# Memory attention and a sticky mixture of experts on one Trainium2 core: Phi's maximum spread by a transpose, and a new table of places

## The chip, the core and the metric

The program runs on one core of one Trainium2 chip. A core has engines that work side by side, each through its own list of instructions in order: TensorE (PE, matrix products; its weight loads are shown as PEld), VectorE (DVE), ScalarE (ACT), GpSimd (POOL) and SyncE (SP), which here issues nearly all transfers between main memory and the core. They wait for one another through semaphores. PE reads SBUF, the core's working memory, and writes PSUM, the accumulation memory; ACT and DVE read PSUM, POOL doesn't. The metric is device time in microseconds (us) of one execution.

## The reference, cut to what matters

```python
# attention with a memory: q, k, v [8 batches, 8 heads, 576, 64], phi [8, 8, 576, 32]
a = exp(phi - phi.max(axis=2)); a = a / (a.sum(axis=2) + 1e-9)      # over the 576 tokens
k_m = einsum('bhsm,bhsd->bhmd', a, k); v_m = einsum('bhsm,bhsd->bhmd', a, v)
attn = softmax(q @ k_m.T / 8)                                       # 576 x 32 per head
x = (attn @ v_m), heads side by side                                # [8, 576, 512]
# experts: w_gate [512, 8], w_local [512, 1], w1 [8, 512, 1024], w2 [8, 1024, 512]
for b in batches:
    for s in tokens:
        e = argmax(x[b, s] @ w_gate) if s == 0 or sigmoid(x[b, s] @ w_local) < 0.5 else previous e
        out[b, s] = softmax(x[b, s] @ w_gate)[e] * (relu(x[b, s] @ w1[e]) @ w2[e])
```

The maximum that is taken off Phi runs over the 576 tokens, for each head and memory column. All data are float32.

## The kernel before, in words

Tokens of a batch lie over the 128 partitions: two halves of 64 partitions hold two groups of heads (NG = 2, four heads each, HG = 4), nine tokens to a partition. The work of one batch falls into three parts.

- **Phi's part.** `f_colmax` (L312) takes the maximum over a partition's nine tokens on DVE; `f_pm` (L344) transposes the 128 x 128 result on PE; `f_mc` (L348) reduces it to one number for each column and half, a tile `mc` of 128 x 2; `f_pm2` (L352) brings it back to all partitions: for each half it multiplies `mc`'s column, read 64 times over as the stationary operand, with the identity, which writes 64 partitions of PSUM. `f_cx` (L359) copies the result to SBUF on ACT, `f_sub` takes it off Phi on POOL in two pieces, `f_exp` is ACT's exponential. `f_asum` (L372) adds over a partition's tokens on DVE.
- **Keys, values and scores.** `f_pkv` (L389) multiplies exp(Phi) with keys and values, `f_sums` (L404) with ones; `f_rinv` and `f_kvn` divide, `f_pT` and `f_kvT` transpose, `f_pgg` and `f_ggt` multiply the result into the gate's weights. The queries come in two parts, "a" and "z", of nine blocks of 32 tokens: DVE transposes them (`k_qT`, L474), PE makes the scores (`k_psc`, L499), DVE and ACT the softmax (`k_turn` to `k_mul`), and a transpose on DVE (`k_at`, L553) writes them into `at`, of which there is one buffer; `k_store` stores it to memory (`att_d`).
- **Experts.** The first token's expert is the batch's own: `c_pl` ("pl0", L575) and `c_choice` find it, SP reads its number and loads w1 and w2 in halves of 1 MB, with three buffers. Since x = attn @ v_m, w1 is first multiplied by v_m (`w_pg`, L780, two halves "pg 0" and "pg 1", split into a high and a low part by `w_G`), and the hidden layer is attn times this product (`hidden`, L804): three passes of float32r products on the full array, three buffers of PSUM, ACT's relu and DVE's remainder behind each. `w_split` (L768) splits w2 into high and low parts, on ACT and POOL. `second` (L839) and `second_turned` (L897) make the output, again with three products for each piece. `g_pl` ("g pl", L600) and the steps behind it decide by a scan on DVE which tokens stay with which expert. Tokens with another expert than the batch's first are done in a loop behind all batches (`rest`, L983).

The products use PE's array in different tiles, which the profile prints: 128*128 in `hidden`, `second` and the transposes, 64*32 in pkv, sums, pgg, psc and pg, 128*64 in pm2, 128*32 in g pl, 128*1 in pl0.

**What sets the order.** The schedule is manual: the program is emitted in the order in which the steps are called, and each engine works through its share in this order. The start of the program (`start`, L1145) is written out and holds the first part of batches 0 and 1. After it, the loop at L1235 goes through the experts' products of each batch. Each piece of `hidden`, `second` and `second_turned` yields its length in table time, 37.8 us (END) for a batch; behind each piece the loop emits all steps whose place lies below the time reached, in order of place:

```python
for x in moe(sts[b]):
    now += x
    while places and places[0][0] <= min(now, (b + 1) * END - 0.01):
        _, _, name, n = places.pop(0)
        STEPS[name](sts[n])
```

PLACES (L25 to L111) has 85 rows, one for each kind of step, with a place for each batch; among them are the loads ("phi", "kv", "q", "w1", "w2"), the stores and the splits. A place is table time, which counts the experts' products alone; the steps between take time of their own. So the work on batch b + 1 lies between the products of batch b. A new number changes an engine's list only if the step passes another step of that engine or a piece of the experts' work.

Of the kernel before, what the change touches and what calls it, by code (L numbers as in the profile page):

```python
# [8 lines left out]
F32 = mybir.dt.float32  # L9
F32R = mybir.dt.float32r  # L10
I32 = mybir.dt.int32
AF = mybir.ActivationFunctionType
# [10 lines left out]

END = 37.8
PLACES = {  # L25
    "phi": {2: 1.9, 3: 37.2, 4: 67.4, 5: 94, 6: 129.3, 7: 167.1},
    "kv": {2: 6.06, 3: 36.1, 4: 67.5, 5: 94.1, 6: 129.4, 7: 167.2},
    "colmax": {2: 21.6, 3: 55.3, 4: 80.6, 5: 109.2, 6: 147, 7: 184.8},
# [8 lines left out]
    "asum": {2: 31, 3: 64.8, 4: 92.7, 5: 128.3, 6: 165.5, 7: 203.9},  # L37
    "pkv": {1: 1.56, 2: 34.5, 3: 67.3, 4: 93.6, 5: 128.9, 6: 166.7, 7: 204.5},
    "sums": {1: 3.2, 2: 35.7, 3: 68.6, 4: 94.4, 5: 129.5, 6: 167.8, 7: 205.6},
    "rinv": {1: 3.2, 2: 35.8, 3: 69.6, 4: 95.1, 5: 131.3, 6: 169.1, 7: 207.8},  # L40
    "kvn": {1: 7.7, 2: 36.8, 3: 70.1, 4: 95.5, 5: 131.7, 6: 170, 7: 208.2},
    "pT": {1: 9.2, 2: 38, 3: 71.6, 4: 97.5, 5: 133.7, 6: 171.5, 7: 209.3},
    "kvT": {1: 9.8, 2: 38.3, 3: 71.9, 4: 97.5, 5: 133.7, 6: 171.5, 7: 209.3},
    "kv store": {0: 18.79, 1: 11.1, 2: 41.9, 3: 73.7, 4: 98.7, 5: 136.3, 6: 174.1, 7: 211.9},
    "pgg": {1: 9.9, 2: 39.5, 3: 73.1, 4: 99, 5: 135.8, 6: 173, 7: 210.8},
    "ggt": {1: 9.9, 2: 41.6, 3: 73.2, 4: 99.7, 5: 135.9, 6: 173.7, 7: 211.5},
# [15 lines left out]
    "choice": {1: 22.1, 2: 53.4, 3: 86.6, 4: 112.5, 5: 150.3, 6: 187.5, 7: 227.3},  # L62
    "expert": {1: 22.3, 2: 53.9, 3: 87.6, 4: 112.7, 5: 150.5, 6: 187.7, 7: 227.5},
# [36 lines left out]
    "store": {0: 39.3, 1: 79.4, 2: 116.9, 3: 153.6, 4: 189.4, 5: 227.2, 6: 265},  # L100
    "pairs": {0: 29.3},
    "list": {7: 278.9},
# [8 lines left out]
}  # L111


# [1 line left out]
def tile_memattn_stickymoe(  # L115
# [12 lines left out]
    nc = tc.nc  # L128
    B, H, S, D = q.shape
    M = phi.shape[3]  # L130
    E, DM, F = w1.shape
    P = 128
    HG = 4
    NG = H // HG
# [10 lines left out]
    psml = ctx.enter_context(tc.tile_pool(name="psml", bufs=2))  # L145
# [9 lines left out]
    ident = const.tile([P, P], F32, name="ident")  # L155
# [192 lines left out]
    def f_mc(st):  # L348
        st.mc = psml.tile([P, NG], F32, tag="mc", name="mc")
        nc.vector.tensor_reduce(out=st.mc, in_=st.pm.rearrange("x (g p) -> x g p", g=NG), axis=AX.X, op=ALU.max)  # L350

    def f_pm2(st):  # L352
        st.pm = ps_a.tile([P, P], F32, tag="pa", name="pm")
        for g in range(NG):
            nc.tensor.matmul(
                st.pm[half[g]], lhsT=st.mc[:, g : g + 1].to_broadcast([P, D]), rhs=ident, start=True, stop=True
            )
# [678 lines left out]
    a, z = PARTS  # L1036
# [15 lines left out]
    def al(st, p):  # L1052
# [8 lines left out]
        "colmax": f_colmax,  # L1061
        "pm": f_pm,
        "mc": f_mc,
        "pm2": f_pm2,
        "cx": f_cx,
        "sub 0": lambda st: f_sub(st, 0),
# [78 lines left out]
    def start():  # L1145
# [14 lines left out]
        f_pm(s)  # L1160
        warm(1)
        f_mc(s)
        f_pm2(s)
        warm(14)
        f_cx(s)
# [28 lines left out]
        f_pm(n)  # L1194
        warm(3)
        f_mc(n)
        c_pl(s)
        c_choice(s)
# [5 lines left out]

        k_psc(s, p)
        f_pm2(n)
        f_cx(n)
        f_sub(n, 1)
# [23 lines left out]
    with tc.manual_schedule():  # L1232
        start()
        places = sorted((x, i, name, n) for i, (name, row) in enumerate(PLACES.items()) for n, x in row.items())
        for b in range(B):  # L1235
            now = b * END
# [38 lines left out]
```

## Time and profile before

| | |
|---|---|
| median of 3 runs | 417.17 us (416.37 to 418.63) |
| profiled execution | 416.56 us, its span 414.8 us |
| PE | busy 395.0 us, 95% of the span, 4195 products |
| PE weight loads | 326.7 us, 79% |
| DVE | 284.4 us, 69%, 714 instructions |
| ACT | 177.8 us, 43%, 427 instructions |
| POOL | 150.9 us, 36% |
| DMA | 82.58 MB, 199 GB/s on average |
| chain that ended last | PE 79%, DMA 11%, DVE 5% of the span |
| clock granted to PE | 0.999 of full speed |

In the rows of the timeline the first two numbers are the start, in us from the span's start, and the length of an instruction (or of a run of equal ones, with their count behind "x"). Then come the engine, the line of the kernel, the operation, "out<-in", for PE the tile of the array, and the shape. A bracket gives the engine's idle time before it and what ended it. "SPq" is SP's queue, whose instructions issue transfers. Matmuls of PE overlap, and their ends are modelled; the distance from one start to the next says more than the length. Rows of stages give a stretch, its length, then for each engine the busy time and the number of instructions.

### The profile page before, as it was taken

Reading aid. Unit: us, or ns where it says so; the run is one execution under the profiler, and the core shown is the slowest. Engines: PE = TensorE matmul, PEld = TensorE weight load, DVE = VectorE, ACT = ScalarE, POOL = GpSimd, SP = SyncE. Lnnn points to the kernel's source line nnn. Section 1 sums busy time; section 2 is a strip of 40 time slices with the busy share of each in tenths; the row PEclk is TensorE's granted clock in tenths of the full one; section 3 lists DMA queues with packets and bytes.
Section 4 is the critical chain, followed back from the end, with each engine's and each line's share of the span. In section 5 each row is a group of like instructions: output and inputs, shape, how many; then the busy total and the mean of one; then the engine's idle time right before and its main releaser. Section 6 shows DMA issues by size and latency. Waiting matters only on the chain.

```text
span 414.8 us, 10606 instructions
## 1 busy us (share of the span) xinstructions
PE 395.0 (95%) x4195; PEld 326.7 (79%) x4195; DVE 284.4 (69%) x714; ACT 177.8 (43%) x427; POOL 150.9 (36%) x162
## 2 busy tenths in 40 slices
PE   8778898999999989999999999999999999999994
PEld 2546866798777977699778997789878996899884
DVE  4487788878976797886759767777757676625300
ACT  2154652436442744435541564336541564146010
POOL 3024541536241744038510681029410660156000
PEclk9999999999999999999999999999999999999999
DMA  8969793999197939798789198965974087202011
GB/s 238 286 224 291 167 372 122 199 283 378 31 351 127 371 131 246 174 379 299 228 162 399 37 300 152 297 244 164 241 134 170 2 246 253 82 0 65 25 40 55
DMA packets 115445, 82.58 MB, mean 199 GB/s; under 512 B 69616, under 2 KB 89088, under 8 KB 115392
## 3 DMA queue, kind: packets, MB, share of 16 engines
q1 hardware_dynamic: 115328, 81.84, 66.4%
q8 instruction: 35, 0.57, 0.6%
q14 instruction: 18, 0.15, 0.1%
q0 software_dynamic: 64, 0.02, 0.1%
HBM read 66.60 MB, written 15.24 MB: 197 GB/s over the span
## 4 chain that ended last, share of the span: by engine, by line
PE 79%; DMA 11%; DVE 5%; issue 1%; SPq 1%; ACT 1%; DVEq 0%
PE ph L819 22%; PE po L907 8%; PE po L857 8%; PE po L908 7%; PE po L909 7%; PE po L859 7%; PE po L858 7%; DMA att_d<-at 6%; DMA kv_t<-in_v_dram 5%; PE pkv L396 4%; PE pg L787 3%; PE psc L507 2%; PE pl L604 1%; DVE h L829 1%; PE po L881 1%
## 5 line engine op out<-in xcount | busy, mean ns | idle before, releaser
L777 POOL TENSOR_TENSOR w2l<-raw,w2h 128x512 fp32r<-128x512 f32 x64 | 82.0, 1303 | 31.2 <-ACT w2h L776 23.5
L819 PE MATMUL ph<-ah,Gh 128*128 128x256 f32 (+1 forms) x256 | 74.5, 306 | 1.4 <-DVE h L829 1.3
L829 DVE SCALAR_TENSOR_TENSOR h<-ph,h 128x320 fp32r<-128x320 f32 (+2 forms) x104 | 52.7, 519 | 31.9 <-ACT h L827 31.5
L819 PE MATMUL ph<-ah,Gl 128*128 128x256 f32 (+1 forms) x256 | 71.6, 295 | 0.0
L907 PE MATMUL po<-h,w2l 128*128 128x320 f32 x224 | 71.5, 319 | 0.0
L909 PE MATMUL po<-h,w2h 128*128 128x320 f32 x224 | 69.2, 309 | 0.0
L908 PE MATMUL po<-h,w2h 128*128 128x320 f32 x224 | 69.2, 309 | 0.0
L827 ACT ACTIVATE h<-ph 128x320 fp32r<-128x320 f32 (+1 forms) x96 | 46.4, 489 | 44.7 <-PE ph L819 44.4
L857 PE MATMUL po<-w2h,h 128*128 128x512 f32 (+1 forms) x152 | 60.7, 399 | 0.0
L914 POOL TENSOR_TENSOR oT<-oT,gT 128x320 f32<-128x320 f32 x28 | 20.7, 741 | 104.3 <-DVE oT L913 97.4
L859 PE MATMUL po<-w2h,h 128*128 128x512 f32 (+1 forms) x152 | 57.8, 380 | 0.0
L858 PE MATMUL po<-w2l,h 128*128 128x512 f32 (+1 forms) x152 | 57.7, 379 | 0.0
L819 PE MATMUL ph<-al,Gh 128*128 128x256 f32 (+1 forms) x256 | 54.8, 295 | 0.0
L819 PEld LDWEIGHTS ph<-ah,Gh 128*128 128x128 f32 x256 | 48.1, 188 | 7.6 <-issue 3.6
L819 PEld LDWEIGHTS ph<-ah,Gl 128*128 128x128 f32 x256 | 48.2, 188 | 0.0
L563 POOL TENSOR_TENSOR al<-at,ah 128x576 fp32r<-128x576 f32 (+1 forms) x18 | 23.1, 1289 | 64.7 <-ACT ah L559 42.8
L907 PEld LDWEIGHTS po<-h,w2l 128*128 128x128 f32 x224 | 42.0, 188 | 5.6 <-issue 5.2
L776 ACT ACTIVATE w2h<-raw 128x512 fp32r<-128x512 f32 x64 | 38.4, 625 | 11.9 <-PE po L909 10.1
L908 PEld LDWEIGHTS po<-h,w2h 128*128 128x128 f32 x224 | 42.1, 188 | 0.2
L909 PEld LDWEIGHTS po<-h,w2h 128*128 128x128 f32 x224 | 42.1, 188 | 0.0
L819 PEld LDWEIGHTS ph<-al,Gh 128*128 128x128 f32 x256 | 41.1, 188 | 0.1
L857 PEld LDWEIGHTS po<-w2h,h 128*128 128x128 f32 x152 | 28.6, 188 | 14.3 <-issue 9.4
(153 smaller groups left out, 578.6 us busy)
## 6 DMA issues: line engine op xcount, KB each, us to landing
raw<-in_moe_w_dram SPq DMA_DIRECT2D x34, 512.0 KB, 6.2
raw<-in_moe_w_dram SPq DMA_DIRECT2D x15, 1024.0 KB, 6.9
kv_t<-in_k_dram SPq DMA_DIRECT2D x7, 1152.0 KB, 8.7
kv_t<-in_v_dram SPq DMA_DIRECT2D x7, 1152.0 KB, 11.2
q_t<-in_q_dram SPq DMA_DIRECT2D x112, 72.0 KB, 3.3
att_d<-at SPq DMA_DIRECT2D x8, 576.0 KB, 9.8
out_dram<-oT SPq DMA_DIRECT2D x28, 160.0 KB, 5.6
out_dram<-ot SPq DMA_DIRECT2D x17, 256.0 KB, 6.0
```

The source lines that it names most:

```text
L563: (eng or nc.gpsimd).tensor_tensor(out=st.al[:, gs, ss], in0=st.at[:, gs, ss], in1=st.ah[:, gs, ss], op=ALU.subtract)
L776: nc.scalar.activation(h, src, AF.Copy)
L777: nc.gpsimd.tensor_tensor(out=l, in0=src, in1=h, op=ALU.subtract)
L819: nc.tensor.matmul(pv[:, c - c0], lhsT=lt[:, g, cs], rhs=rt[:, g, s0 : s0 + n], start=(i == 0), stop=(i == 5),)
L827: nc.scalar.activation(hc[:, :, 0:n], pv, AF.Relu)
L829: nc.vector.scalar_tensor_tensor(out=hc[:, :, o : o + z - a], in0=pv[:, :, a:z], scalar=0.0, in1=hc[:, :, a:z], op0=ALU.max, op1=ALU.subtract,
L857: nc.tensor.matmul(po[:, c0:c1], lhsT=h[:, c, th], rhs=hi, start=(c == 0), stop=False)
L858: nc.tensor.matmul(po[:, c0:c1], lhsT=h[:, c, th], rhs=lo, start=False, stop=False)
L859: nc.tensor.matmul(po[:, c0:c1], lhsT=h[:, c, tl], rhs=hi, start=False, stop=(c == FC - 1))
L907: nc.tensor.matmul(po[:, 0:n], lhsT=lo, rhs=h[:, c, 0:n], start=(c == 0), stop=False)
L908: nc.tensor.matmul(po[:, 0:n], lhsT=hi, rhs=h[:, c, 0:n], start=False, stop=False)
L909: nc.tensor.matmul(po[:, 0:n], lhsT=hi, rhs=h[:, c, n : 2 * n], start=False, stop=(c == FC - 1))
```

## The change

Two things are changed.

The spread of Phi's maximum, in batches 1 to 7: `f_mc` adds an activation that writes `mc`'s two columns 64 times each into a tile `mcw` of 128 x 128, and `f_pm2` transposes it by one product on the full array, where it had two products on an array tile of 128*64 (four instructions of PE). Batch 0 keeps the old way.

```diff
     def f_mc(st):
         st.mc = psml.tile([P, NG], F32, tag="mc", name="mc")
         nc.vector.tensor_reduce(out=st.mc, in_=st.pm.rearrange("x (g p) -> x g p", g=NG), axis=AX.X, op=ALU.max)
+        if st.b:
+            st.mcw = psml.tile([P, NG, D], F32, tag="mcw", name="mcw", bufs=1)
+            nc.scalar.activation(st.mcw, st.mc.unsqueeze(2).to_broadcast([P, NG, D]), AF.Copy)
 
     def f_pm2(st):
         st.pm = ps_a.tile([P, P], F32, tag="pa", name="pm")
+        if st.b:
+            nc.tensor.transpose(st.pm, st.mcw.rearrange("x g p -> x (g p)"), ident)
+            return
         for g in range(NG):
             nc.tensor.matmul(
                 st.pm[half[g]], lhsT=st.mc[:, g : g + 1].to_broadcast([P, D]), rhs=ident, start=True, stop=True
             )
```

The table PLACES: 61 of the 85 rows get new numbers, many of them changed by a few tenths. The rows that move products of PE, loads, or steps which the text below speaks of:

```diff
-    "kv": {2: 6.06, 3: 36.1, 4: 67.5, 5: 94.1, 6: 129.4, 7: 167.2},
+    "kv": {2: 6.06, 3: 36.1, 4: 74.8, 5: 98.6, 6: 133.9, 7: 171.7},
-    "pkv": {1: 1.56, 2: 34.5, 3: 67.3, 4: 93.6, 5: 128.9, 6: 166.7, 7: 204.5},
-    "sums": {1: 3.2, 2: 35.7, 3: 68.6, 4: 94.4, 5: 129.5, 6: 167.8, 7: 205.6},
+    "pkv": {1: 1.52, 2: 34.49, 3: 70.3, 4: 93.6, 5: 127.71, 6: 165.81, 7: 204.5},
+    "sums": {1: 1.52, 2: 34.49, 3: 70.3, 4: 94.4, 5: 127.71, 6: 165.81, 7: 204.51},
-    "pgg": {1: 9.9, 2: 39.5, 3: 73.1, 4: 99, 5: 135.8, 6: 173, 7: 210.8},
+    "pgg": {1: 9.9, 2: 39.5, 3: 73.1, 4: 100.59, 5: 138.8, 6: 176, 7: 213.8},
-    "pl0": {1: 20, 2: 53.3, 3: 86.6, 4: 111.6, 5: 149.4, 6: 186.6, 7: 226.4},
+    "pl0": {1: 20, 2: 54.8, 3: 86.6, 4: 111, 5: 148.8, 6: 186, 7: 225.8},
-    "z psc": {1: 24.2, 2: 51.9, 3: 88.3, 4: 119.4, 5: 157.2, 6: 190.5, 7: 232.8},
+    "z psc": {1: 24.2, 2: 53.29, 3: 89, 4: 119.4, 5: 157.2, 6: 190.5, 7: 232.8},
-    "at store": {0: 8.78, 1: 31.2, 2: 67.5, 3: 91.6, 4: 140.3, 5: 179.9, 6: 211.4, 7: 253.7},
+    "at store": {0: 6.78, 1: 33.2, 2: 67.5, 3: 91.6, 4: 140.3, 5: 179.9, 6: 211.4, 7: 253.7},
-    "w2 0": {1: 22.7, 2: 57.9, 3: 93.2, 4: 121.1, 5: 161.2, 6: 199, 7: 235.9},
+    "w2 0": {1: 22.7, 2: 57.9, 3: 93.2, 4: 122, 5: 162.1, 6: 199.9, 7: 236.8},
-    "pg 1": {0: 0.13, 1: 32.7, 2: 71.5, 3: 97.6, 4: 132.9, 5: 170.1, 6: 205.9, 7: 242.8},
-    "G 1": {0: 0.13, 1: 32.8, 2: 71.6, 3: 98.3, 4: 135, 5: 171.1, 6: 206.9, 7: 244.1},
+    "pg 1": {0: 0.51, 1: 34.5, 2: 71.5, 3: 97.6, 4: 132.9, 5: 165.81, 6: 213.79, 7: 246.79},
+    "G 1": {0: 0.51, 1: 34.78, 2: 71.6, 3: 98.3, 4: 135, 5: 171.1, 6: 213.79, 7: 246.79},
```

The rows "pm", "mc", "pm2", "g pl" and "q" keep their places, and the splits of batch 6 move back by up to 4.5 us. The loads of w1 keep theirs but for batch 2 (1.5 us later).

More of the change, by code (lines that the diff above doesn't have):

```diff
@@ L25 @@
 PLACES = {
-    "phi": {2: 1.9, 3: 37.2, 4: 67.4, 5: 94, 6: 129.3, 7: 167.1},
-    "kv": {2: 6.06, 3: 36.1, 4: 67.5, 5: 94.1, 6: 129.4, 7: 167.2},
-    "colmax": {2: 21.6, 3: 55.3, 4: 80.6, 5: 109.2, 6: 147, 7: 184.8},
+    "phi": {2: 1.3, 3: 37.2, 4: 70.3, 5: 94, 6: 129.3, 7: 167.1},
+    "kv": {2: 6.06, 3: 36.1, 4: 74.8, 5: 98.6, 6: 133.9, 7: 171.7},
+    "colmax": {2: 21.6, 3: 55.3, 4: 80, 5: 109.8, 6: 147.6, 7: 185.4},
     "pm": {2: 24.1, 3: 59.1, 4: 84.8, 5: 114, 6: 151.8, 7: 189.6},
@@ L31 @@
     "pm2": {2: 27.1, 3: 60.6, 4: 89.4, 5: 117.2, 6: 155, 7: 192.8},
[3 rows of a table removed]
[3 rows of a table added]
     "exp 0": {2: 29.4, 3: 63.8, 4: 90.5, 5: 125.6, 6: 163.7, 7: 201.5},
     "exp 1": {2: 30.9, 3: 63.8, 4: 91.4, 5: 126.8, 6: 164.6, 7: 202.4},
-    "asum": {2: 31, 3: 64.8, 4: 92.7, 5: 128.3, 6: 165.5, 7: 203.9},
-    "pkv": {1: 1.56, 2: 34.5, 3: 67.3, 4: 93.6, 5: 128.9, 6: 166.7, 7: 204.5},
-    "sums": {1: 3.2, 2: 35.7, 3: 68.6, 4: 94.4, 5: 129.5, 6: 167.8, 7: 205.6},
-    "rinv": {1: 3.2, 2: 35.8, 3: 69.6, 4: 95.1, 5: 131.3, 6: 169.1, 7: 207.8},
@@ L41 @@
-    "kvn": {1: 7.7, 2: 36.8, 3: 70.1, 4: 95.5, 5: 131.7, 6: 170, 7: 208.2},
+    "asum": {2: 31, 3: 64.8, 4: 92.7, 5: 127.71, 6: 165.5, 7: 203.9},
+    "pkv": {1: 1.52, 2: 34.49, 3: 70.3, 4: 93.6, 5: 127.71, 6: 165.81, 7: 204.5},
+    "sums": {1: 1.52, 2: 34.49, 3: 70.3, 4: 94.4, 5: 127.71, 6: 165.81, 7: 204.51},
+    "rinv": {1: 2.9, 2: 35.8, 3: 70.3, 4: 95.1, 5: 131.3, 6: 169.1, 7: 207.8},
+    "kvn": {1: 7.4, 2: 36.8, 3: 70.3, 4: 95.5, 5: 131.7, 6: 170, 7: 208.2},
     "pT": {1: 9.2, 2: 38, 3: 71.6, 4: 97.5, 5: 133.7, 6: 171.5, 7: 209.3},
-    "kvT": {1: 9.8, 2: 38.3, 3: 71.9, 4: 97.5, 5: 133.7, 6: 171.5, 7: 209.3},
@@ L44 @@
-    "kv store": {0: 18.79, 1: 11.1, 2: 41.9, 3: 73.7, 4: 98.7, 5: 136.3, 6: 174.1, 7: 211.9},
-    "pgg": {1: 9.9, 2: 39.5, 3: 73.1, 4: 99, 5: 135.8, 6: 173, 7: 210.8},
-    "ggt": {1: 9.9, 2: 41.6, 3: 73.2, 4: 99.7, 5: 135.9, 6: 173.7, 7: 211.5},
+    "kvT": {1: 9.8, 2: 38, 3: 71.9, 4: 97.5, 5: 133.7, 6: 171.5, 7: 209.3},
+    "kv store": {0: 18.79, 1: 11.1, 2: 41.9, 3: 76, 4: 98.7, 5: 136.3, 6: 174.1, 7: 211.9},
+    "pgg": {1: 9.9, 2: 39.5, 3: 73.1, 4: 100.59, 5: 138.8, 6: 176, 7: 213.8},
+    "ggt": {1: 9.9, 2: 41.6, 3: 75.5, 4: 100.59, 5: 138.8, 6: 176, 7: 213.8},
@@ L47 @@
     "q": {1: 1.15, 2: 22.6, 3: 59.6, 4: 88.7, 5: 124.3, 6: 162.1, 7: 199.9},
[3 rows of a table removed]
[3 rows of a table added]
     "a turn": {1: 14.1, 2: 46.1, 3: 75.6, 4: 103.2, 5: 141.3, 6: 178.8, 7: 217.7},
[2 rows of a table removed]
[2 rows of a table added]
     "a exp": {1: 15.2, 2: 49.8, 3: 80.8, 4: 104.7, 5: 142.8, 6: 180.3, 7: 219.2},
     "a sum": {1: 17.6, 2: 49.8, 3: 82, 4: 105.8, 5: 143.9, 6: 181.4, 7: 220.3},
[3 rows of a table removed]
[3 rows of a table added]
     "a ah": {1: 18.8, 2: 52.8, 3: 85.1, 4: 108.9, 5: 147, 6: 183.9, 7: 223.4},
[2 rows of a table removed]
-    "choice": {1: 22.1, 2: 53.4, 3: 86.6, 4: 112.5, 5: 150.3, 6: 187.5, 7: 227.3},
-    "expert": {1: 22.3, 2: 53.9, 3: 87.6, 4: 112.7, 5: 150.5, 6: 187.7, 7: 227.5},
[18 rows of a table removed]
[2 rows of a table added]
@@ L82 @@
+    "choice": {1: 22.1, 2: 54.9, 3: 86.6, 4: 111.3, 5: 149.1, 6: 186.3, 7: 226.1},
+    "expert": {1: 22.3, 2: 55.4, 3: 87.6, 4: 112.7, 5: 150.5, 6: 188, 7: 227.5},
[18 rows of a table added]
     "pg 0": {1: 30.7, 2: 66.7, 3: 96.2, 4: 127.7, 5: 165.8, 6: 203.6, 7: 240.5},
[3 rows of a table removed]
[3 rows of a table added]
     "g pl": {0: 4.27, 1: 30.9, 2: 61.6, 3: 93.6, 4: 132, 5: 169.8, 6: 207.1, 7: 246.8},
[3 rows of a table removed]
[3 rows of a table added]
     "g exp": {0: 9.2, 1: 33, 2: 65.7, 3: 96.3, 4: 135.3, 5: 173.1, 6: 210.9, 7: 250.1},
```

82 rows, old and new, of the table PLACES are left out of this document.

## The prediction

> **What bounds the kernel now.** I read the page first, then a table of the engines' busy time by stage, then the timeline of TensorE (PE) around each small product, and last the rows of what PE waits for.
>
> ```profile
> span 414.8 us, 10606 instructions
> ```
>
> The profiled execution took 416.56 us: this span and 1.76 us around it. The stages, cut where a batch's expert begins (columns: span, PE, weight loads, DVE, ACT, POOL busy, granted clock, DMA share, GB/s):
>
> ```profile
> 38.60:88.80 50.20, 46.77 (x524) 38.22 (x518) 40.49 (x105) 22.04 (x57) 20.34 (x24) 1.00 0.80 212
> 187.90:234.60 46.70, 46.70 (x510) 39.71 (x509) 35.03 (x84) 21.30 (x52) 18.56 (x17) 1.00 0.77 239
> ```
>
> In the later batch PE is busy for all 46.70 us; in the first it waits for 3.4 of 50.2. From then on PE's own order is the time: what shortens PE's list shortens the run, unless another engine comes late for it. Up to there it is otherwise:
>
> ```profile
> 63.21 0.78 DVE L555 STREAM_TRANSPOSE at<-sc 128x576 f32<-128x576 f32 x1 [0.94 <-DMA att_d<-at]
> ```
> ```profile
> 64.13 0.24 PE L578 MATMUL pl<-ggt,at 128*1 128x8 f32 x4 [1.11 <-DVE at L555]
> ```
>
> PE stands 1.11 us before batch 1's pl0, because the transpose into `at` waits for the store of batch 0's `at`. In SP's queue this store keeps its neighbours under the new table. So what PE gains before 64 us is lost in that wait, and a loss of up to 1.11 us there is hidden too. I count nothing before 64 us.
>
> **The change part by part.** First the spread of Phi's maximum, before: four products on an array tile of 128*64, inside full-array products of 256 columns.
>
> ```profile
> 191.90 0.40 PE L819 MATMUL ph<-al,Gh 128*128 128x256 f32 x2
> 192.22 0.44 PE L355 MATMUL pm<-ident,mc 128*64 128x128 f32 x4
> 192.59 0.39 PE L819 MATMUL ph<-ah,Gh 128*128 128x256 f32 x1
> 192.82 0.28 PE L819 MATMUL ph<-ah,Gl 128*128 128x256 f32 x1
> ```
>
> The nearest row to the transpose that replaces them is the transpose of the column maxima, the same 128x128 on the full array:
>
> ```profile
> 188.83 0.28 PE L819 MATMUL ph<-ah,Gl 128*128 128x256 f32 x1
> 188.95 0.40 PE L819 MATMUL ph<-al,Gh 128*128 128x256 f32 x2
> 189.19 0.27 PE L346 MATMUL pm<-ident,cm 128*128 128x128 f32 x1
> 189.21 0.36 PE L819 MATMUL ph<-ah,Gh 128*128 128x256 f32 x1
> 189.41 0.28 PE L819 MATMUL ph<-ah,Gl 128*128 128x256 f32 x1
> ```
>
> I count starts, since matmuls overlap: 188.83 to 188.95 gives 0.12 for one of these products. From 191.90 to 192.82 are three such steps, 0.35, in 0.92: the spread costs 0.57. From 188.95 to 189.41 are three in 0.46: the transpose costs 0.11. The difference is 0.46 a batch. Six batches (2 to 7) lie behind 64 us: 6 x 0.46 = 2.8. The other end takes the transpose by its duration of 0.27, 0.30 a batch and 1.8 in all; I take 2.8, because the cost in a stream is what the neighbours' starts show. Batch 1's spread lies in the start, ahead of the wait above, and counts for nothing.
>
> The Trainium skill, "TensorE: Matmul & The Clock Gate", Part 4: PE-mode transpose, gives about 275 ns for a 128x128 transpose inside a kernel, mostly access latency. The row's duration of 0.27 agrees with it, the starts beside it do not pay it; by that figure the sum would lose 1.0.
>
> Second, the table. Where steps now stand together I need the price of a product that stands alone. Batch 2's pkv and sums apart:
>
> ```profile
> 83.30 2.25 PE L396 MATMUL pkv<-kv_t,phi_t 64*32 64x128 f32 x144
> 85.48 0.41 PE L907 MATMUL po<-h,w2l 128*128 128x320 f32 x1
> ...
> 86.32 0.31 PE L909 MATMUL po<-h,w2h 128*128 128x320 f32 x1
> 86.56 0.27 PE L407 MATMUL pkv<-ones,asum 64*32 64x1 f32 x16
> 86.75 0.41 PE L907 MATMUL po<-h,w2l 128*128 128x320 f32 x1
> 87.00 0.30 PE L908 MATMUL po<-h,w2h 128*128 128x320 f32 x1
> 87.15 0.31 PE L909 MATMUL po<-h,w2h 128*128 128x320 f32 x1
> ```
>
> and batch 5's pg 0 alone, then its pkv and sums, which already adjoin:
>
> ```profile
> 204.54 0.39 PE L859 MATMUL po<-w2h,h 128*128 128x512 f32 x1
> 204.86 1.09 PE L787 MATMUL pg<-raw,kvT 64*32 64x512 f32 x16
> 205.88 0.50 PE L857 MATMUL po<-w2h,h 128*128 128x512 f32 x1
> 206.22 0.39 PE L858 MATMUL po<-w2l,h 128*128 128x512 f32 x1
> 206.44 0.40 PE L859 MATMUL po<-w2h,h 128*128 128x512 f32 x1
> ...
> 207.46 2.25 PE L396 MATMUL pkv<-kv_t,phi_t 64*32 64x128 f32 x144
> 209.45 0.29 PE L407 MATMUL pkv<-ones,asum 64*32 64x1 f32 x16
> 209.68 0.50 PE L857 MATMUL po<-w2h,h 128*128 128x512 f32 x1
> ```
>
> Sums alone: 86.32 to 87.00 is 0.68, less two steps of 0.15 (87.00 to 87.15), so 0.39. Pkv alone runs 2.18 to the next product, pkv with sums 2.22: there sums cost 0.04. Adjoining saves 0.35, for two changes of array tile less. Pg alone: 204.54 to 206.22 is 1.68, less two steps of 0.23 (206.22 to 206.44), so 1.22, of which 1.02 is its own pace (204.86 to 205.88); at least 0.20 lies in its two changes. One change costs 0.10 to 0.175.
>
> The Trainium skill, "TensorEngine Tiling (Array Packing)", Tiling Modes, Key Properties, says that changing the tiling mode drains the engine and that changing the tile alone doesn't. The 0.39 against 0.04 agrees.
>
> I ordered both tables by their numbers, as the loop at the end of the program does, and counted changes of array tile on PE behind batch 1's pl0: 118 before, 93 after. Twelve go with the spread, already counted. Four go with sums 2 and 3 that join pkv: 2 x 0.35 = 0.7. Nine go elsewhere: pg 1 of batch 1 behind pkv and sums (2), pg 0 of batches 4 and 5 ahead of pkv (4), pg 1 of batches 5 and 6 moved from g pl to pkv or pgg (1 each), pg 1 of batch 7 to g pl (1). Nine at 0.10 to 0.175 are 0.9 to 1.6; I take 1.2, the middle, since pg stands between the two rows in size. Sums.1 joins too, but ahead of 64 us.
>
> Third, what the change adds: one activation a batch, and a link in the chain mc, mcw, pm2, cx. Batch 3 has the shortest of these links:
>
> ```profile
> 114.96 0.23 DVE L350 TENSOR_REDUCE mc<-pm 128x2 f32<-128x128 f32 x1
> ```
> ```profile
> 115.69 0.44 PE L355 MATMUL pm<-ident,mc 128*64 128x128 f32 x4
> ```
> ```profile
> 115.80 0.69 ACT L944 ACTIVATE ot<-po,gt 128x512 f32<-128x512 f32 x1 [3.38 <-PE po L859]
> 116.38 0.27 ACT L361 ACTIVATE cx<-pm 128x128 f32<-128x128 f32 x1
> ```
>
> The widened copy has the shape of cx's, 0.27. ACT stands idle for 3.38 before 115.80, so mcw can run from 115.19 to 115.46, ahead of PE's 115.69. What is queued behind it on ACT is the eviction of ot, whose products end after it. With the handing over I charge 0.2 for all six. In batches 4 to 7 relus and splits are queued behind mcw, and PE waits for relus only through three buffers of PSUM: no charge, unless mc itself is late (below).
>
> Fourth, moved steps on other queues. The kv loads of batches 4 to 7 are issued 4.5 to 7.3 us later by the table, behind stores and w2 loads; pkv 4 still stands 18.8 us behind its load, and the landing takes:
>
> ```profile
> kv_t<-in_v_dram SPq DMA_DIRECT2D x7, 1152.0 KB, 11.2
> ```
>
> so nothing is charged. For batches 6 and 7 q goes ahead of w2 0 in SP's queue. That bears on batch 6's pl0, where the same wait as at 64 us recurs:
>
> ```profile
> 247.69 12.78 SPq L253 DMA_DIRECT2D q_t<-in_q_dram  x16
> ```
> ```profile
> 278.87 0.78 DVE L555 STREAM_TRANSPOSE at<-sc 128x576 f32<-128x576 f32 x1 [1.74 <-DMA att_d<-at]
> ```
> ```profile
> 279.71 0.24 PE L578 MATMUL pl<-ggt,at 128*1 128x8 f32 x4 [0.52 <-DVE at L555]
> ```
>
> Sixteen issues of q take SP 12.78, and the store of `at` comes behind them. Started earlier, they let that store out earlier. pl0 itself moves one step of 0.88 ahead (six products of 0.147 by the program's own yield). Between a gain of 0.52 and a loss of 0.88 I take a gain of 0.4: DVE is ready 1.74 before the store lets it go on, so a store that comes earlier by that much leaves room for both moves.
>
> The sum: 2.8 + 0.7 + 1.2 + 0.4 - 0.2 = 4.9. 416.56 - 4.9 = 411.7. The median of the runs, 417.17, lies 0.6 above the profiled one; the sum from there gives 412.3. I say 412.0.
>
> **Rivals.** *Only the removed products count.* If a transpose costs its 0.27 and a change of tile beside pg nothing, 1.8 + 0.7 - 0.2 = 2.3 is left: 416.56 - 2.3 = 414.3. For it: durations are what the rows print. Against it: the two starts around 189.2.
>
> *The saved time turns into waits.* If DVE or the store of `at` sets each batch's pace, PE only waits longer at pl0, or for relus' buffers; what is saved behind the last such wait at 279.7 remains: batch 7's spread 0.46 and two changes of tile, 0.3; 416.56 - 0.8 = 415.8, no change. For it: both waits for that store, and DVE's 40.49 of 50.20 in the early stage. Against it: from 187.9 PE has no idle time, and DVE only 35.03 of 46.70.
>
> *Slower: PE stands at pm2 for mcw.* ACT takes its list in order, and mcw comes behind whatever the table has put there:
>
> ```profile
> 189.94 1.14 ACT L776 ACTIVATE w2h<-raw 128x512 fp32r<-128x512 f32 x2
> ```
>
> With two splits ahead (1.14) and then its own 0.27, the copy would come 1.4 late where nothing is to spare, and PE would stand for it in each of six batches: 8.4 against 4.9, 416.56 + 3.5 = 420.1. It decides from 4.9/6 = 0.8 of mean wait at pm2. Against it: between 115.19 and 115.69 ACT was idle.
>
> **How the numbers follow.** About 0.5% (2.1 us) is what a measurement of this kernel can tell from no change. Forecast 0.62, only-removed 0.12, waits 0.17, slower 0.09. The first two are faster by over 0.5%, the second narrowly: 0.74. The waits are no change: 0.17. Slower: 0.09. The range goes down to 408.0, where each change of tile costs 0.175 (0.4 more) and PE's idle time of 3.4 in the first stage goes as well; up to 416.5 it holds the rival of less gain and most of the one of the waits.
>
> **What would show it.** Right: pm2 as one transpose, 0.1 between its neighbours' starts; sums 2 and 3 directly behind pkv; PE's busy time down by about 5 and its idle time unchanged; stages from 187.9 on at 46.0 or less. Wrong: PE idle at pm2 with ACT as releaser, longer waits at pl0 for `at`, or pg behind pkv still paying its 0.2. A change of more than 2 us in the first 64 us would break my claim that nothing counts there.

## The result, and the profile after

The changed kernel takes 412.19 us (median of 7 executions, 411.31 to 414.49), the kernel before beside it 417.17 (7 executions, 416.32 to 418.93). The ratio is 0.9882, with a 95% interval of 0.9848 to 0.9917: faster by 1.2%. The prediction was 412.0, within 408.0 to 416.5. The profiled execution of the changed kernel took 414.21, near the upper end of its own executions, so the two traces lie only 2.4 apart; a second trace, taken below, took 412.06.

The page of the changed kernel, span and PE's busy time:

```profile
span 412.4 us, 10572 instructions
...
PE 391.7 (95%) x4170; PEld 327.3 (79%) x4174; DVE 284.2 (69%) x714; ACT 179.4 (44%) x434; POOL 151.3 (37%) x162
```

PE's busy time fell by 3.3 (395.0 before; 391.3 in the second trace), where the prediction said about 5. Busy time is a poor witness here: a group of products that stands waiting in its middle, as some below, is partly counted as busy.

The spread of batch 5 in the changed kernel, on PE's timeline:

```profile
190.51 0.40 PE L825 MATMUL ph<-al,Gh 128*128 128x256 f32 x2
190.75 0.27 PE L358 MATMUL pm<-ident,mcw 128*128 128x128 f32 x1
190.77 0.36 PE L825 MATMUL ph<-ah,Gh 128*128 128x256 f32 x1
190.97 0.28 PE L825 MATMUL ph<-ah,Gl 128*128 128x256 f32 x1
191.09 0.28 PE L825 MATMUL ph<-ah,Gh 128*128 128x256 f32 x1
```

By the starts: 190.51 to 190.97 is 0.46 for three products of 0.12 (190.97 to 191.09) and the transpose, so the transpose costs 0.10. The prediction took 0.11 from the neighbour's row, and 0.57 for the old spread. The Trainium skill's figure in "TensorE: Matmul & The Clock Gate", Part 4: PE-mode transpose, some 275 ns (measured with bfloat16 data), is again the row's duration and not what the stream pays.

Batch 2's pkv with sums, and pg 1 of batch 1 behind them:

```profile
82.31 2.25 PE L402 MATMUL pkv<-kv_t,phi_t 64*32 64x128 f32 x144
84.30 0.25 PE L413 MATMUL pkv<-ones,asum 64*32 64x1 f32 x12
84.39 0.61 PE L793 MATMUL pg<-raw,kvT 64*32 64x512 f32 x1
...
84.49 1.14 PE L793 MATMUL pg<-raw,kvT 64*32 64x512 f32 x15
85.56 0.42 PE L913 MATMUL po<-h,w2l 128*128 128x320 f32 x1
```

The three follow one another with no product of the experts between them. To price such a block I use one rule from here on: from the start of the last full-array product ahead of it to the start of the second one behind it, less the steps these two take in a run of their own. This block costs 3.45 by that rule. In the kernel before, pkv cost 2.38, sums 0.39 and pg about 1.22 apart.

The wait at batch 1's pl0 on the timeline of the changed kernel, and the stage of batch 3's experts (columns as in the prediction):

```profile
63.88 0.78 DVE L561 STREAM_TRANSPOSE at<-sc 128x576 f32<-128x576 f32 x1 [1.81 <-DMA att_d<-at]
...
64.80 0.24 PE L584 MATMUL pl<-ggt,at 128*1 128x8 f32 x4 [1.20 <-DVE at L561]
```
```profile
186.57:233.51 46.94, 46.50 (x506) 39.98 (x505) 35.51 (x86) 21.60 (x53) 19.68 (x18) 1.00 0.84 256
```

The wait at pl0 stayed (1.11 before, 1.20 now), as forecast. But the stage from 186.57 takes 46.94, longer than its 46.70 before, though PE's list in it is shorter: a wait has appeared that the prediction does not name. The experiments trace it.

### The profile page after: what moved, and what is told of

Its sections match the earlier page's. It is cut to its first block, busy times and chain, and to the rows that moved or that the text cites. A ratio compares the mean times of both kernels' runs of the same rounds, so it can differ in the third digit from the quotient of the medians.

```text
span 412.4 us, 10572 instructions
## 1 busy us (share of the span) xinstructions
PE 391.7 (95%) x4170; PEld 327.3 (79%) x4174; DVE 284.2 (69%) x714; ACT 179.4 (44%) x434; POOL 151.3 (37%) x162
## 4 chain that ended last, share of the span: by engine, by line
PE 68%; DMA 11%; SPq 11%; DVE 6%; issue 2%; ACT 1%; DVEq 0%; ACTq 0%
PE ph L825 19%; SPq L253 7%; PE po L863 7%; PE po L913 7%; PE po L865 6%; PE po L864 6%; PE po L915 6%; PE po L914 6%; DMA att_d<-at 6%; PE pkv L402 3%; PE pg L793 3%; DMA raw<-in_moe_w_dram 3%; DMA kv_t<-in_v_dram 2%; PE psc L513 2%; DVE h L835 1%
```

## The experiments

Twelve runs were made, in four sets, each set beside the kernel before on one chip. "Profiled" is the one execution that left the trace.

| kernel | median, us (executions) | ratio to before, 95% interval | profiled |
|---|---|---|---|
| spread alone | 416.14 (12) | 0.9978, 0.9951 to 1.0004 | 418.12 |
| table alone | 413.75 (6) | 0.9905, 0.9869 to 0.9942 | 413.70 |
| widened copy four times | 416.06 (12) | 0.9961, 0.9935 to 0.9986 | 416.91 |
| one small product for each group | 437.10 (2) | 1.0472, 1.0350 to 1.0594 | 435.96 |
| one full-array product for each group | 422.53 (2) | 1.0123, 1.0020 to 1.0227 | 422.98 |
| eight small products for each group | 455.99 (2) | 1.0925, 1.0781 to 1.1069 | 454.33 |
| whole change again | 411.59 (5) | 0.9857, 0.9834 to 0.9881 | 412.06 |
| loads behind the store of `at` | 410.51 (6) | 0.9846, 0.9812 to 0.9881 | 410.91 |
| the same, maximum of batch 4 in halves | 410.82 (5) | 0.9843, 0.9817 to 0.9869 | 414.71 |
| pkv 3 at its old place | 414.73 (8) | 0.9948, 0.9920 to 0.9976 | 414.79 |
| spread alone, again | 416.25 (10) | 0.9979, 0.9957 to 1.0002 | 415.57 |
| before, again | 416.25 (1) | | 416.25 |

The standing theory was the prediction's: PE's own list is the time, the spread gives 2.8 of it, the table 1.9, and the added link costs 0.2 at most. The rivals: waits eat the gain, or PE stands at pm2 for the copy.

### The two parts apart, and the link lengthened

The spread alone, with the old table:

```diff
+        if st.b:
+            st.mcw = psml.tile([P, NG, D], F32, tag="mcw", name="mcw", bufs=1)
+            nc.scalar.activation(st.mcw, st.mc.unsqueeze(2).to_broadcast([P, NG, D]), AF.Copy)
...
+        if st.b:
+            nc.tensor.transpose(st.pm, st.mcw.rearrange("x g p -> x (g p)"), ident)
+            return
```

> The spread by a transpose alone, with the old table. By the prediction's sum (0.46 a batch, six batches behind 64 us, less 0.2 for the longer chain) it gains 2.6 us on the kernel before. If a transpose costs its duration of 0.27, it gains 1.6. If saved time of PE only turns into waits, it gains less than 0.8.

A miss: 416.14 against 417.33 beside it, 1.2 in place of 2.6, and the interval takes in no change.

The table alone is the changed kernel without these lines.

> The new table alone, with the old spread. By the prediction's sum (0.7 for sums 2 and 3, 1.2 for nine changes of array tile, 0.4 for batch 6's pl0) it gains 2.3 us. If a change of tile beside pg costs nothing, it gains 0.7. The trace of the changed kernel still has PE waiting 0.75 at batch 6's pl0, so that I now expect 1.9 without the 0.4.

Also a miss, to the other side: 413.75 against 417.33, 3.6 faster.

The link made longer: the widened copy is written four times over in place of once.

```diff
-            nc.scalar.activation(st.mcw, st.mc.unsqueeze(2).to_broadcast([P, NG, D]), AF.Copy)
+            for _ in range(4):
+                nc.scalar.activation(st.mcw, st.mc.unsqueeze(2).to_broadcast([P, NG, D]), AF.Copy)
```

> The changed kernel with the copy into mcw done four times, so that the link from mc to the transpose is 0.9 us longer in every batch. By the prediction the link has room: in the changed kernel's trace the transpose starts 0.16 behind the copy in batch 3, 0.78 in batch 5, 0.83 in batch 6 and more elsewhere, so that PE stands 0.8 in batch 3, 0.1 to 0.2 in batches 5 and 6: about 1 us slower than the changed kernel. If the link sets the time (the slower rival), 0.9 in each of six batches, 5.6 us slower.

It took 416.06, about 4 above the changed kernel: more than the 1 of the first case, less than the 5.6 of the second. Its timeline at batch 3's spread:

```profile
114.39 1.33 ACT L354 ACTIVATE mcw<-mc 128x128 f32<-128x128 f32 x4 [2.81 <-DVE mc L350]
...
115.78 0.33 PE L359 MATMUL pm<-ident,mcw 128*128 128x128 f32 x1 [0.75 <-ACT mcw L354]
```

and the same place in the changed kernel:

```profile
114.68 0.31 ACT L353 ACTIVATE mcw<-mc 128x128 f32<-128x128 f32 x1 [2.79 <-DVE mc L350]
...
115.15 0.27 PE L358 MATMUL pm<-ident,mcw 128*128 128x128 f32 x1
```

One copy ends at 114.99, 0.16 ahead of the transpose: PE does not wait, but there is no more room than that. With 0.93 more (three copies of 0.31) the starts around pm2 lengthen by 1.0, 0.6, 0.3 and 0.3 in batches 3 to 6, and not in 2 and 7. So the six links have room for one copy, not for four. These 2.2 are about half of the 4. The rest, against the second trace of the changed kernel (below), is waiting of PE at other places, which no theory had named yet: batch 6's pl0, behind the store of `at`, costs 2.30 by the starts in place of 0.72, and the scores of batches 4 and 5 cost 0.4 and 0.3 more.

### What a change of array tile costs

96 products that nobody reads, of one column, each ahead of a group of `hidden` products (whose first product overwrites what they wrote):

```diff
+                for _ in range(1):
+                    nc.tensor.matmul(ph[0:32, 0:1], lhsT=wz[0:64, 0:32], rhs=wz[0:64, 0:1], start=True, stop=True)
```

> The changed kernel with one product of no use ahead of each group of the hidden layer (96 in all): bfloat16 zeros, one column, on an array tile of 64*32, into a bank of PSUM that the group's own first product overwrites. If a change of array tile costs 0.10 to 0.175 us, each pays two: 96 x 0.20 to 0.35 = 19 to 34 us slower than the changed kernel. If the cost is the product's own, it is what the next kernel's full-array product costs.

> The same with the product of no use on the full array, one column too, so that no tile changes. If changes of tile are the cost, this adds only the product and its weight load, below 0.1 each, under 10 us in all. If small products as such are the cost, it adds as much as the small tile did.

> The same with eight products on the 64*32 tile ahead of each group: 768 products, but no more changes of tile than with one. If the change is the cost, it adds at 0.01 for each further product (the pace of pkv's products) 96 x 7 x 0.01 = 7 us to what one does; all eight take the same tile, so that up to 0.1 each, 67 us, is possible where one waits for the other. If each small product pays by itself, it adds eight times what one does.

The second has `ph[0:128, 0:1]`, `wz[0:128, 0:128]` and `wz[0:128, 0:1]`, so the full array; the third has eight of the small ones in place of one. Against the changed kernel's 412.19 (measured in another set; the kernel before beside it was at 417.17, here at 416.89) the first is slower by 24.9, which is 0.26 for each small product, the second by 10.3, 0.11 for each. The third adds 18.9 to the first for 672 more products, 0.028 each. Timelines of the first and the second:

```profile
240.07 0.31 PE L917 MATMUL po<-h,w2h 128*128 128x320 f32 x1
240.31 0.17 PE L822 MATMUL ph<-wz 64*32 64x1 bf16 x1
240.41 0.39 PE L827 MATMUL ph<-ah,Gh 128*128 128x256 f32 x1
240.63 0.28 PE L827 MATMUL ph<-ah,Gl 128*128 128x256 f32 x1
```
```profile
240.94 0.40 PE L827 MATMUL ph<-al,Gh 128*128 128x256 f32 x2
241.18 0.18 PE L822 MATMUL ph<-wz 128*128 128x1 bf16 x1
241.21 0.39 PE L827 MATMUL ph<-ah,Gh 128*128 128x320 f32 x1
241.45 0.31 PE L827 MATMUL ph<-ah,Gl 128*128 128x320 f32 x1
```

Ahead of the small product PE loses 0.24 to its start in place of 0.15, and the first product behind it takes 0.22 in place of 0.12. Behind the full-array one the follower starts 0.03 later, and its own step takes 0.24 in place of 0.15. By the starts in the three traces the medians are 0.30 for a small product, 0.12 for a full-array one and 0.025 for a further small one, so the times of two executions each are not far off. A small product that follows another small one costs almost nothing; if it would cost as little alone, a pair of changes is 0.26 - 0.03 = 0.23, 0.115 for each (0.14 by the starts), within the prediction's 0.10 to 0.175. If one takes off what the full-array product costs, which changes no tile, it is 0.15, 0.075 for each (0.09 by the starts), below that range. That a change costs something is shown; its size only between these two. The rule of the Trainium skill, "TensorEngine Tiling (Array Packing)", Key Properties, that a change of mode drains the engine, agrees with 0.26 against 0.028; it states no price.

### The whole again, and the first 64 us

The changed kernel again, and two edits of it that aim at two waits in its trace. First, the loads of batch 2's Phi, keys and values go behind the store of batch 0's `at` in SP's queue, and the store of batch 5's goes earlier:

```diff
-    "phi": {2: 1.3, ...
-    "kv": {2: 6.06, ...
+    "phi": {2: 6.85, ...
+    "kv": {2: 6.9, ...
-    "at store": {..., 5: 179.9, ...
+    "at store": {..., 5: 169, ...
```

> The changed kernel once more, beside the two below. 5.0 us faster than before, and in the trace the waits of the first 64 us and at batch 6's pl0 again, if they belong to the order and not to one execution.

> The changed kernel with the store of at ahead of phi 2 and kv 2 (batch 0) and ahead of w2 1 and kv 7 (batch 5) in SP's queue. If PE's waits at pl0 of batches 1 and 6 are waits for that store behind other transfers, both go: 1.36 - 0.10 and 0.75 - 0.10, together up to 1.9 us faster than the changed kernel. If something else comes as late (the scores' chain on DVE, 0.9 before the store in batch 1), 0.9 at most at the first.

The whole took 411.59. The edit took 410.51, faster by 1.1 by medians where up to 1.9 was hoped for, and the intervals overlap. In its trace the wait is gone; SP's rows, and DVE and PE:

```profile
48.02 0.41 SPq L578 DMA_DIRECT2D att_d<-at  x1
48.52 0.38 SPq L231 DMA_DIRECT2D phi_t<-in_phi_dram  x1
```
```profile
61.69 0.78 DVE L561 STREAM_TRANSPOSE at<-sc 128x576 f32<-128x576 f32 x1
...
63.26 0.25 PE L584 MATMUL pl<-ggt,at 128*1 128x8 f32 x4
```

The store left 2.1 earlier than in the trace of the whole (50.15), DVE no longer waits for it, and the block of pl0 costs 0.37 in place of 1.58 by the starts. So the prediction's cause of that wait is right, and in the block it was worth 1.2. Batch 6's pl0, for which the store of batch 5 was moved, costs 0.37 in place of 0.72. How much of this the whole run keeps, the medians do not settle: the first 64 us of one kernel alone, to the mark used below, moved by 2.3 between two executions (spread alone). Second, the same with the maximum of batch 4 (2.25 us on DVE in one piece, for which PE stands 1.5) cut in two:

```diff
-    "colmax": {2: 21.6, 3: 55.3, 4: 80, ...
+    "colmax a": {4: 80},
+    "colmax b": {4: 81.8},
```

> The same, and batch 4's column maxima in two halves of 1.1 us with products of the hidden layer between them. If PE's wait of 1.5 at 146 us is for relus of DVE behind the one reduce of 2.2, about 1.0 of it goes, beside b1. If DVE is full there anyway, nothing.

410.82: no gain. By the starts PE's one wait of 1.50 became one of 0.48 and one of 1.20; the second half stands ahead of the next remainder as the whole did.

### Why the spread alone gains so little and the table so much: batch 3's pkv and batch 4's scores

> The changed kernel with four numbers set back to the old table: batch 3's pkv from 70.3 to 67.3, its sums to 68.6, rinv to 69.6, kvn to 70.1. My theory: what the table alone brought beyond its changes of array tile (3.6 us by medians against 1.9 to 2.3 from the working) is in part a pause inside batch 3's pkv, which stands in the profile of the kernel before and of the spread alone (130 or 139 of 144 products, then 0.5 to 0.6 us without a releaser) and not in the profiles where pkv 3 stands later. Then this kernel's pkv 3 shows the pause again, and the run is slower than the changed kernel by the pause, 0.8 to 1.0, and by sums that stand alone, 0.35: about 1.2 us, near 413.2. The rival, that the pause has nothing to do with the place: pkv 3 costs 2.38 or less and only 0.35 is lost, near 412.3.

> The spread alone with the old table, once more, for a second trace. Seen so far: 416.1 in place of the 414.6 expected from the old kernel's profiled execution; the stretches that hold pm2 were shorter by 0.4 to 0.46 each, and 1.5 us went between batch 3's output and batch 3's hidden layer, where the scores of batch 4 waited 0.81 for the transpose of queries whose load had landed 2.5 us late for DVE. Theory: the shorter list of PE runs into the load of batch 4's queries, whose 16 issues take SP 15 us. Then this trace shows the wait at batch 4's scores again, by 0.3 or more, and 5 or 6 stretches shorter by 0.4 to 0.46. Rival: that wait is chance and comes and goes from one execution to the next; then here the scores of batch 4 cost their 0.84 and the end is 2.0 or more us before the old kernel's.

> The kernel before, once more, for a second trace of it. How far do two executions of the same kernel differ at the places that wait for transfers: pl0 of batches 1 and 6, the scores of batch 4? Theory of the link between PE's list and the loads: with the longest list of the kernels, batch 4's scores find their queries transposed (0.84, no wait) here as well. Rival, chance alone: a wait of 0.5 or more there in this execution too. The pause inside batch 3's pkv should be here again (0.4 or more) if it belongs to the old place.

The first sets four numbers back; the others are kernels from above once more.

```diff
-    "pkv": {..., 3: 70.3, ...    "sums": {..., 3: 70.3, ...    "rinv": {..., 3: 70.3, ...    "kvn": {..., 3: 70.3, ...
+    "pkv": {..., 3: 67.3, ...    "sums": {..., 3: 68.6, ...    "rinv": {..., 3: 69.6, ...    "kvn": {..., 3: 70.1, ...
```

PE's timeline at batch 3's pkv in the kernel before, in the changed one, and in the changed one with pkv 3 back:

```profile
124.49 2.15 PE L396 MATMUL pkv<-kv_t,phi_t 64*32 64x128 f32 x130
127.11 0.45 PE L396 MATMUL pkv<-kv_t,phi_t 64*32 64x128 f32 x14 [0.47 <-issue]
```
```profile
127.11 2.25 PE L402 MATMUL pkv<-kv_t,phi_t 64*32 64x128 f32 x144
```
```profile
122.68 2.20 PE L402 MATMUL pkv<-kv_t,phi_t 64*32 64x128 f32 x138
125.38 0.42 PE L402 MATMUL pkv<-kv_t,phi_t 64*32 64x128 f32 x6 [0.51 <-issue]
```

At the old place pkv 3 pauses in all five traces that have it there (blocks of 3.01 to 3.35), at the new place in none (2.41 with sums). The pause is worth 0.8 (3.19 + 0.39 for sums, against 2.41 for both, less the 0.35 of the joint) and goes with the place; what PE waits for in it, no trace shows ("issue"). One thing in the traces goes with it. The DMA queue that the pages call "instruction" moves a packet of 16 KB, in 1.5 us, near this place. In the five blocks with a pause the packet starts 0.2 to 0.5 ahead of pkv's first product and lands 1.0 to 1.3 behind it; in the 61 other blocks of pkv behind 64 us (all traces but those of the added small products) the last such packet has landed 0.3 or more ahead, and the next starts 2.0 or more behind. That PE's own instructions come late there is the rival that this points to; no run tests it. Set back, pkv and sums cost 3.25 + 0.39 = 3.64 in place of 2.41, the 1.2 of the theory. The time rose by more, 2.5 to 3.1 by medians; its trace shows waits of 1.80 at batch 4's scores and a block of 1.34 at batch 6's pl0 besides, and the second trace of the changed kernel has 0.34 and 0.72 there.

There lies the other half. The timeline of the spread alone, second trace, at those scores:

```profile
174.71 0.69 PE L513 MATMUL psc<-qT,kvT 64*32 64x288 f32 x8
175.10 0.78 DVE L486 STREAM_TRANSPOSE qT<-q_t 128x576 f32<-128x576 f32 x1 [2.21 <-DMA q_t<-in_q_dram]
...
175.94 0.69 PE L513 MATMUL psc<-qT,kvT 64*32 64x288 f32 x8 [0.54 <-DVE qT L486]
```

PE does half of the scores, then waits for DVE, which waits for the queries' load. In both traces of the kernel before, this block costs its 0.84; here it costs 2.05, and 2.32 in the first trace of the spread alone. So the theory holds, not chance. Why does the load come late? I followed it back. The issue stands in SP's queue behind w1 for batch 3's expert, and w1 waits for the number of that expert; in both traces of the spread alone the first issue then waits 0.3 more for a step of the softmax on DVE, which stands behind the choice in DVE's list. The timeline of the kernel before, around batch 3's pl0:

```profile
152.33 0.24 PE L578 MATMUL pl<-ggt,at 128*1 128x8 f32 x4
...
152.94 0.25 DVE L350 TENSOR_REDUCE mc<-pm 128x2 f32<-128x128 f32 x1
153.11 0.87 DVE L829 SCALAR_TENSOR_TENSOR h<-ph,h 128x320 fp32r<-128x320 f32 x2
...
154.50 0.14 DVE L597 TENSOR_SCALAR ei<-c 1x1 int32<-1x1 f32 x1
```

and that of the spread alone, second trace:

```profile
150.82 0.25 PE L584 MATMUL pl<-ggt,at 128*1 128x8 f32 x4
...
151.42 0.26 DVE L350 TENSOR_REDUCE mc<-pm 128x2 f32<-128x128 f32 x1
151.77 0.31 ACT L353 ACTIVATE mcw<-mc 128x128 f32<-128x128 f32 x1 [2.28 <-DVE mc L350]
152.08 0.68 ACT L565 ACTIVATE ah<-at 128x576 fp32r<-128x576 f32 x1
152.67 1.07 ACT L833 ACTIVATE h<-ph 128x320 fp32r<-128x320 f32 x3
...
153.12 0.89 DVE L835 SCALAR_TENSOR_TENSOR h<-ph,h 128x320 fp32r<-128x320 f32 x2 [1.44 <-ACT h L833]
...
154.54 0.14 DVE L603 TENSOR_SCALAR ei<-c 1x1 int32<-1x1 f32 x1
```

The new activation stands at the head of ACT's list for 2.28, until `mc` is there. Behind it stand `ah` and the relus. DVE's remainder waits 1.44 for such a relu, and behind the remainder in DVE's list stand the four steps that choose the expert. In the kernel before, ACT's list had nothing there that waited for `mc`. The chain of work that ended last, as the profile follows it back, takes this way in both traces of the spread alone: `mc`, the copy, `ah`, a relu, the remainder, the four steps of the choice, DVE's softmax, the queries' issues and load, DVE's transpose, the scores. From pl0 to the issue of w1, and on to the scores:

| | pl0 of batch 3 to its w1's issue | w1's issue to batch 4's scores | wait in both parts (a and z) of these scores |
|---|---|---|---|
| before, two traces | 3.15, 3.16 | 20.60, 20.58 | 0, 0 |
| spread alone, two traces | 4.70, 4.70 | 19.20, 19.19 | 1.63, 1.75 |
| table alone | 3.17 | 21.53 | 0 |
| whole change, two traces | 4.05, 4.05 | 20.48, 20.48 | 1.91, 0.34 |
| copy four times | 4.95 | 20.17 | 0.73 |

(The first two columns are differences of starts; the third is the cost of the two blocks less 2 x 0.84.) The first column repeats within 0.01 from trace to trace of one kernel. The spread adds 1.55 to it under the old table and 0.88 under the new one, which has the maximum of batch 4 earlier, so that `mc` comes 0.08 ahead of pl0 and no longer 0.60 behind it. And four copies add 0.90 to the whole change's 4.05, which is what three more copies last (0.93). That run was made for another question, but it settles this one: the copy stands in the way of the choice of the expert.

The third column swings where the load is tight. SP takes between 13.90 and 15.91 for the 16 issues of batch 4's queries in the two traces of the kernel before alone, and up to 16.07 in the others; the kernel before had room for that (1.15 in one trace, 0.11 in the other, from the end of DVE's transpose to the scores), the spread alone has not. What makes these issues longer or shorter is open. The wait in part z (1.11 in the changed kernel's first trace, 0.34 in its second) runs through a load of w2 that SP issues later in the same queue, ACT's split, the relu behind it and DVE. In the first trace of the changed kernel the chain that ended last (start, length, piece) begins this stretch at the same copy:

```profile
150.55 0.31 ACT mcw L353
150.86 0.68 ACT ah L565
151.54 0.34 ACT h L833
151.90 0.89 DVE h L835 x2
...
156.88 0.53 SPq L253
...
180.55 11.21 DMA raw<-in_moe_w_dram
191.79 0.63 ACT w2h L782
192.42 0.50 ACT h L833
...
194.37 0.69 PE psc L513 x8
```

So the copy is on the way to this wait too, but not alone: this load of w2 is issued 30.29 behind batch 3's pl0, where the two traces of the kernel before have 27.06 and 29.06. Of that 0.9 is the later choice; 2.2 against the one trace and 0.2 against the other are SP's longer issues (16.07).

The spread alone loses at two more places near by. Batch 4's pm2 gains it 0.20 in place of 0.46, although the copy ended 2.4 ahead: in both traces the transpose starts 0.15 behind the end of the choice's second step, which reads pl0, and pm2 takes its place in PSUM from the same three buffers as pl0. That it waits for that buffer is argued from these times; the rows name no releaser. And pkv 4 waits 0.3 for exp(Phi) on ACT.

The forecast of batch 6's pl0 is tested too: the two traces of the kernel before have it at 0.96 and 0.37 by the starts, those of the whole change at 1.03 and 0.72.

## Why the prediction was right, point by point

- **The sum behind 64 us.** I count what PE does from the 49th output product of batch 0 (67.16 before) to its last product. The table has changes against the first trace of the kernel before, us.

| | spread alone, two traces | table alone | whole, two traces |
|---|---|---|---|
| PE's list: spread 2.8, joints 1.9 | -2.8, -2.8 | -1.9 | -4.7, -4.7 |
| pause in pkv 3 (block of 3.19 before) | +0.2, +0.1 | -0.8 | -0.8, -0.8 |
| waits at batch 4's scores | +1.6, +1.7 | 0 | +1.9, +0.3 |
| pl0 of batches 2 and 6 (0.54 and 0.96 before) | -0.4, -0.4 | -0.7 | -0.1, -0.4 |
| pm2 and pkv of batch 4, g pl of batch 3 | +0.6, +0.6 | +0.1 | +0.4, +0.4 |
| sum | -0.8, -0.8 | -3.3 | -3.3, -5.2 |
| measured | -0.75, -0.75 | -3.54 | -3.42, -5.23 |

  It closes to 0.1 for the spread alone and the whole change; for the table alone 0.2 stays unplaced. (There, under the old spread, pm2 of batch 4 comes directly behind scores, which saves 0.2 more.) The first row is the prediction's, confirmed below; the other rows are the blocks' costs by the starts, less those in the first trace of the kernel before. The second trace of the kernel before is itself 0.78 shorter than the first over this stretch, 0.59 of it at batch 6's pl0 and 0.19 in the pause, so against it the spread alone gains nothing, and the whole change 2.64 and 4.45.
- **Spread, 2.8: right on PE.** 0.10 a transpose, 0.46 a batch. In the second trace of the spread alone, five of the stretches that hold pm2 (batches 2, 3, 5, 6, 7) are shorter by 0.42 to 0.46; batch 4's gains 0.20, as said above. **Joints, 0.7 + 1.2: right.** Sums in pkv's block cost 0.03 (2.41 against 2.38); pg 1 of batch 1 saved 2.42 + 1.22 - 3.45 = 0.19, and the other joints of pg, reckoned alike, 0.34 (batch 4), 0.33 (5), 0.16 and 0.21 (6, 7), 1.23 together, 0.14 for each of the nine changes. The traces have 118 and 93 changes of array tile behind batch 1's pl0, as counted.
- **Batch 6's pl0, 0.4: wrong.** A term of 0.4 was read from one trace of a place that moves by 0.6 between two executions of one kernel.
- **The pause in pkv 3, 0.8: not in the prediction**, though its row stands in the trace of before. The step that failed is the pricing of "sums 2 and 3" by batch 2's rows for both: batch 3's own rows held 0.8 more.
- **The link, -0.2: the step that failed is** "In batches 4 to 7 relus and splits are queued behind mcw, and PE waits for relus only through three buffers of PSUM: no charge, unless mc itself is late (below)". With one copy PE never waits for `mcw` at pm2, and there the step is right; the 0.2 charged for the link was not paid there. `mc` is late indeed, but below the prediction asks only what that does to PE at pm2. DVE waits for relus as well, and behind them in DVE's list stand the steps that choose the expert, whose number SP's loads wait for: 0.88 on that path, which PE feels 20 us and more later as a wait of 0.3 to 1.9, by how long SP's issues last in that execution.
- **Nothing before 64 us: held.** The mark at 67.16 moved by +0.69 and +0.29, less than the 2.3 by which two executions of one kernel differ there, and the wait at pl0 stayed.
- **Stages from 187.9 at 46.0 or less: missed.** 46.94, 46.58 and then 46.11 (46.21, 46.26 and 46.11 in the second trace); the first of them holds the wait of 1.11.
- So that 4.9 came so near the 5.0 of the medians is in part luck: an unseen gain of 0.8 stood against unseen losses, 0.3 to 1.9 at the scores and 0.4 around pkv 4. The likeliest case was the right one; the rival of the waits was partly right too, at a place that it did not name. With the old table it is nearly the whole result.

## What to carry to other kernels

An instruction put into an in-order engine costs its wait as well as its length: list what stands behind it, who waits for that, and go on to the loads that hang on it, even when the engine that sets the time is not among the first to wait. Price a step from its own rows in every batch, and look for pauses in the middle of a run of equal instructions. Parts of a change need not add: the table was worth 3.6 alone, the spread 0.9 (416.14 against 417.33 and 416.25 against 416.93, on average, neither clear of no change), both 5.0. In the traces the table shortened the delay that the spread brought from 1.55 to 0.88; that this makes up the 0.5, the medians are too close to show.

The lowest median is that of the changed kernel with the loads behind the store of `at` (410.51), not clear of the whole change's 411.59. A place for batch 4's copy behind the relus that it held up was not tried.

## What the runs showed of the hardware

- One product of 64*32 with one column between full-array products cost PE 0.26 us, one on the full array 0.11, a further small one behind a small one 0.028 (96 places, two executions each).
- The 16 issues of one batch's queries (72 KB each) took SP 13.90 and 15.91 us in two executions of the same kernel, at the same place in its list.
- A run of 144 equal products paused near its end and took 0.6 to 1.0 us longer in all five traces that have it at one place of the program, and in none that have it 3 us of table time later, with no releaser in the trace; of 66 such runs in these five alone a packet of the "instruction" queue was under way at the start.
